# Retention and a snake feed-forward on one core: idle matmuls thinned among the first tiles, two clearings and a table in other gaps, the third sequence's q loads and turn moved

## The chip, the cores and the metric

The kernel runs on one core of a Trainium2 chip. The time is that of one execution on the device in microseconds, the median of several runs. The profile is taken in a separate execution, whose own time stands beside its span.

## The reference

Retention over B = 4 sequences of S = 768 tokens with H = 8 heads of D = 64, then a feed-forward over all 3072 tokens. Inputs and outputs are float32.

```python
gamma = 1.0 - 2.0 ** (-5.0 - np.arange(H))
for t in range(S):
    state = gamma[None, :, None, None] * state + np.einsum('bhd,bhe->bhde', k[:, :, t], v[:, :, t])
    y[:, :, t] = 1/np.sqrt(D) * np.einsum('bhd,bhde->bhe', q[:, :, t], state)
x = y.transpose(0, 2, 1, 3).reshape(B * S, H * D)      # 3072 x 512
h = x @ w_in                                           # 512 -> 2048
s = np.sin(alpha * h)
out = (h + s * s / (alpha + 1e-09)) @ w_out            # 2048 -> 512
```

## The kernel before

**Tiles.** The recurrence is cut into 24 chunks of 128 tokens, six for each sequence, held in bf16. `order` (`P`) begins with the first chunk of each of the four sequences, called `e0` to `e3`, which need no earlier state; then come chunks 1 to 5 of the first sequence, of the second, the third (P[14] to P[18]) and the fourth. The feed-forward takes the chunks in groups: the first four as group 0, then ten groups of two.

**One chunk.** q and k are turned (on PE for the first chunks by `half_T` and `stage_T`, with a copy out of PSUM by ACT or DVE; later by a transposing DMA on SP's queue, `turn`). `stage_A` makes the scores of q and k on PE, and DVE multiplies them with a mask or the table `dec`. `stage_M` multiplies them with v and adds what the state gives; the result goes to `xT`. `scale_v` multiplies the chunk's v in place by a decay, on POOL, after the products that need it unscaled; `stage_S` and `state` sum the state from it. From the second sequence's second remaining chunk on, "wide" chunks do the same in `burst`, on quarters of PE's array.

**Feed-forward.** A `Slot` multiplies `w_in` with `xT` into `ph` (L567), ACT takes the sine (L570) and its square (L575) or DVE the square, and DVE forms `gT` (L582). `ff_out` multiplies `gT` with `w_out` into `po` (L592); `take` copies it out and stores it from SP (L607).

**Order.** The order of the work on every engine is the order of the program's statements; `tc.manual_schedule()` keeps it. Each engine takes its instructions one after the other, and so does each queue: a load issued by POOL stands behind POOL's tables and scalings, a turn on SP behind the stores. Loads from POOL convert float32 to bf16 on the way; there are eight semaphores for them, so that a load waits for the eighth before it.

**The head.** The code from line 645 to 687 brings e0, e1 and e2 through `half_T`, `stage_A` and `stage_M`, with `idle_work` between the steps: matmuls of a cleared float32 tile `warm` into a PSUM tile `spare` that nobody reads, in units of 128 columns, at most four units in one matmul (the trace shows each of them as a pair). `grow(p)` makes the quarter p of `qg[:, 0]`, a table of decays, on ACT; `decay_table(c)` multiplies the whole of `qg[:, 0]` with `step` (1 on DVE, 2 and 3 on POOL, L223). `s_bd` are two tiles for the state that are cleared on DVE (L648). The last lines of the head are POOL's:

```python
    scale_v(e0, nc.gpsimd)
    decay_table(2, nc.gpsimd)
    decay_table(3, nc.gpsimd)
    load_chunk(e3)
    load_w_out(0)
    load_w_in(2)
```

Group 0's feed-forward follows in an order written out by hand (L754 to L897), which begins with `w_in`'s first two quarters and comes to `w_out`'s first at `F(1, 0, 2)`.

**The groups after.** `phase(g, ...)` runs group g in eight slots of two feature tiles; between them stand the output products of group g - 1 and what `atts[g]` has for the slot: (g, n) is slot n of group g. `score[n]` is the place where the scores of chunk P[n] are made: (3, 1) for P[11], (3, 5) for P[12], (4, 1) for P[13], (4, 5) for P[14]. `turns[n]` is the place of its transposing DMA; P[14]'s stands at `score[13]`. `load_seq(2, ...)` loads the third sequence's chunks 1 to 5 with one DMA for each head and tensor; in POOL's order (L784 to L809) its q loads come after the scalings of e2, P[10] and P[11].

Of the kernel before, what the change touches and what calls it, by code (L numbers as in the profile page):

```python
# [9 lines left out]
BF16 = mybir.dt.bfloat16  # L10
# [5 lines left out]
def kernel(  # L16
# [15 lines left out]
    nc = tc.nc  # L32
    B, H, S, D = q.shape
# [69 lines left out]
    def wide(j):  # L103
        return j >= NCH + 2 and j % NCH > 0

    def load_seq(bt, names="qkv", hs=range(H)):

        cs = [c for c in range(NCH) if wide(bt * NCH + c)]
        nh = 2 * len(cs)
        if "q" in names and hs[0] == 0:  # L110
            raw["seq", bt] = (big.tile([128, nh, 2, NP, D], BF16, name=f"qk_seq{bt}"),
                              big.tile([128, nh, NP, D], BF16, name=f"v_seq{bt}"))
        tqk, tv = raw["seq", bt]
        for name, src in (("q", q), ("k", k), ("v", v)):
            if name not in names:
                continue
            for h in hs:
                r = slice(64 * (h // NP), 64 * (h // NP) + 64)
                x = h % NP ^ h // NP
                o = tv[r, :, h % NP, :] if name == "v" else tqk[r, :, "qk".index(name), x, :]  # L120
                nc.gpsimd.dma_start(out=o, in_=src[bt, h, cs[0] * C:, :].rearrange("(f i) d -> i f d", i=64))  # L121
        for i, c in enumerate(cs):
            j, f = bt * NCH + c, slice(2 * i, 2 * i + 2)
            raw["qk", j], raw["k", j], raw["v", j] = tqk[:, f], tqk[:, f, 1], tv[:, f]
# [26 lines left out]
    def scale_v(j, eng):  # L151
        t, by = raw["v", j], kg
        if wide(j):
            t, by = t.rearrange("i f p d -> i (f p) d"), kgq
        eng.tensor_mul(t, t, by[:, j % NCH, :, None].to_broadcast([128, H, D]))  # L155
# [7 lines left out]

    warm = consts.tile([128, 512], F32, name="warm")
    nc.vector.memset(warm, 0.0)  # L165
    tiny = consts.tile([128, 1], F32, name="tiny")
    nc.scalar.activation(out=tiny, in_=warm[:, 0:1], func=ACTF.Exp)
    lg = consts.tile([128, H], F32, name="lg")
# [60 lines left out]
    s_bd = [big.tile([128, NP, 128], BF16, name=f"s_bd{i}") for i in range(2)]  # L229
# [9 lines left out]
    def turn_half(j, i, pt):  # L239

        t = raw["qk"[i], j]
        for p in range(NP):
            if i == 0 and paired(j):
                for f in range(2):
                    for e in range(2):
                        r = slice(64 * e, 64 * e + 64)
                        nc.tensor.transpose(pt[r, p, 64 * f:64 * f + 64], t[:, 2 * p + e, f, :], ident[:64, :64])
            else:
                nc.tensor.transpose(pt[:, p, :], t[:, 2 * p:2 * p + 2, :].rearrange("p h d -> p (h d)"), ident)  # L249

    def half_T(j, i, eng):

        if i == 0:
            st["qkT", j] = work.tile([128, 2 * NP, 128], BF16, name="qkT", tag="qkT", bufs=6)
        pt = psum.tile([128, NP, 128], BF16, name="pt", tag="mm", bufs=4)
        turn_half(j, i, pt)
        leave_T(j, i, pt, nc.scalar.copy if eng is nc.scalar else nc.vector.tensor_copy)

    def leave_T(j, i, pt, copy):

        o = st["qkT", j][:, i * NP:(i + 1) * NP, :]
        if i == 0 and paired(j):
            o = o.rearrange("d p (i f) -> d p f i", f=2)
            pt = pt.rearrange("d p (f i) -> d p f i", f=2)
        copy(o, pt)
# [39 lines left out]
    def stage_S(j):  # L305
        c = j % NCH
        if c == 0:
            st["ps"] = psum.tile([128, NP, D], F32, name="ps", tag="ps")
        ps = st["ps"]
        for p in range(NP):  # L310
            for e in range(2):
                nc.tensor.matmul(ps[64 * e:64 * e + 64, p, :], raw["k", j][:, 2 * p + e, :], raw["v", j][:, 2 * p + e, :],  # L312
                                 start=(c == 0 and p == 0), stop=True, skip_group_check=True)
        return ps
# [6 lines left out]
    def stage_M(j, tag="ty"):  # L321
        c = j % NCH
        g, i = place[j]
        if g not in xT:
            xT[g] = work.tile([128, KS, sizes[g] * C], BF16, name="xT", tag="xT", bufs=3)
        qkT, aT, vs = st["qkT", j], st["aT", j], raw["v", j]
        py = psum.tile([128, NP, 128], F32, name="py", tag=tag)
        if c > 0:
            for p in range(NP):
                for e in range(2):  # L330
                    r = slice(64 * e, 64 * e + 64)
                    nc.tensor.matmul(py[r, p, :], s_bd[c % 2][:, p, r], qkT[:, p, :],  # L332
                                     start=(p == 0), stop=True, skip_group_check=True)
        for p in range(NP):
            for e in range(2):
                nc.tensor.matmul(py[64 * e:64 * e + 64, p, :], vs[:, 2 * p + e, :], aT[:, e, p, :],  # L336
                                 start=(c == 0 and p == 0), stop=True, skip_group_check=True)
        x = xT[g][:, :, i * C:(i + 1) * C]
        if c == 0:
            nc.scalar.copy(x, py)  # L340
            return
        ps = stage_S(j) if c < NCH - 1 else None
        nc.vector.tensor_mul(x, py, qg[:, c])
        if ps is not None:
            if wide(j + 1):
                swapped(s_b[(c + 1) % 2][0], ps, nc.scalar.copy)
                swapped(s_f[0], ps, nc.vector.tensor_copy)
            else:
                keep_S(j, ps)
# [3 lines left out]
    def halves_M(j):  # L353

        g, i = place[j]
        aT, vs = st["aT", j], raw["v", j]
        for h, (tag, copy) in enumerate((("ps", nc.scalar.copy), ("ty", nc.vector.tensor_copy))):
            idle_work(2 * h)
            py = psum.tile([128, 2, 128], F32, name="py", tag=tag)
            for n in range(2):  # L360
                for e in range(2):
                    p = 2 * h + n
                    nc.tensor.matmul(py[64 * e:64 * e + 64, n, :], vs[:, 2 * p + e, :], aT[:, e, p, :],
                                     start=(n == 0), stop=True, skip_group_check=True)
            copy(xT[g][:, 2 * h:2 * h + 2, i * C:(i + 1) * C], py)
# [4 lines left out]
    def swapped(o, ps, copy):  # L370

        m = NP // 2
        copy(o[:, :m], ps[:, :m])
        for e in range(2):
            copy(o[half(1 - e), m:], ps[half(e), m:])
# [256 lines left out]
    spare = {"ps": psum.tile([128, 512], F32, name="spare", tag="mm", bufs=4)}  # L632

    def idle_work(n):
        while n > 0:
            m = min(n, 4) * 128
            nc.tensor.matmul(spare["ps"][:, :m], warm[:, :128], warm[:, :m], start=True, stop=True)  # L637
            n -= 4

    def grow(p):  # L640
        nc.scalar.activation(out=qg[:, 0, p, :], in_=tio, func=ACTF.Exp, scale=lgp[:, p:p + 1], bias=cscale)


    P = order
    e0, e1, e2, e3 = P[:B]
    idle_work(8)
    for t in s_bd:
        nc.vector.memset(t, 0.0)  # L648
    nc.vector.tensor_copy(raw["q", 0], near["q"])
    half_T(e0, 0, nc.scalar)  # L650
    half_table(0)
    nc.vector.tensor_copy(raw["k", 0], near["k"])
    half_table(1)
    idle_work(3)
    half_T(e0, 1, nc.vector)
    nc.scalar.activation(out=kg, in_=expo, func=ACTF.Exp, scale=-1.0)
    later_tables()
# [5 lines left out]
    grow(1)  # L663
    half_T(e1, 0, nc.scalar)
    nc.scalar.activation(out=kgq, in_=expoq, func=ACTF.Exp, scale=-1.0)
    grow(2)
    idle_work(2)
    half_T(e1, 1, nc.vector)
    nc.tensor.transpose(pal, alpha_row, ident_f)
    nc.scalar.copy(alpha_sb, pal)  # L670
    stage_M(e0)
    stage_A(e1)
    idle_work(2)
    grow(3)
    half_T(e2, 0, nc.scalar)
    idle_work(2)
    half_T(e2, 1, nc.vector)
    nc.scalar.activation(out=tiny, in_=warm[:, 0:1], func=ACTF.Sin)
    stage_M(e1)
    idle_work(1)  # L680
    stage_A(e2, 2)
    idle_work(3)
    halves_M(e2)
    idle_work(3)
    nc.vector.tensor_scalar_add(rec_alpha, alpha_sb, 1e-9)
    nc.vector.reciprocal(rec_alpha, rec_alpha)
    decay_table(1, nc.vector)
# [104 lines left out]
    scale_v(P[9], nc.gpsimd)  # L792
    load_seq(1, "v", range(4, H))
    scale_v(e2, nc.gpsimd)
    for j in P[10:12]:
        scale_v(j, nc.gpsimd)
    load_seq(2, "q")
    scale_v(P[12], nc.gpsimd)
    load_seq(2, "k")
    scale_v(P[13], nc.gpsimd)  # L800
# [97 lines left out]
    score = {6: (1, 1), 7: (1, 3), 8: (2, 0), 9: (2, 2), 10: (2, 5)}  # L898
# [5 lines left out]
    turns = {8: (1, 0), 9: (1, 2), 10: (1, 7), **{n + 2: score[n] for n in range(9, NJ - 2)}}  # L904
# [8 lines left out]
    for n in range(6, NJ + 1):  # L913
# [9 lines left out]
                at(score[n], SK(first))  # L923
        if n >= 18 and n + 1 < NJ:
            at(score[n], lambda j=P[n + 1]: scale_v(j, nc.gpsimd))
    turns[14] = score[13]
    for n, spot in sorted(turns.items()):
        at(spot, X(P[n]))
    phase(1, out_pieces(0, (3,)), atts[1], 2, (0, 6))
# [33 lines left out]
```

## Time and profile before

| | |
|---|---|
| median of 3 runs | 210.32 us (210.24 to 211.41) |
| profiled execution, own time | 211.66 us |
| its span | 209.9 us |
| PE, DVE, ACT, POOL busy | 97%, 76%, 76%, 52% of the span |
| chain that ended last | PE 88%, DMA 6%, POOL 3%, DVE 1% |
| first product with `w_out` on PE | 24.27 us after the span's start |
| idle matmuls (L637) | 22 records, 10.3 us |
| granted clock | 1.00 |

PE's busy time counts from a matmul's start to its modelled end, so a high share alone does not say that PE is at its best; but it says where PE waited. Times in the text count from the span's start. L and a number name a line of the kernel before.

### The profile page before, as it was taken

The numbers are of one execution on the slowest core, as the hardware profiler recorded it, in microseconds if no ns is written. First come the engines' busy times: TensorE is split into PE (matmuls) and PEld (weight loads), VectorE is DVE, ScalarE is ACT, GpSimd is POOL, SyncE is SP. The second block draws the span as 40 slices with busy tenths as digits, with TensorE's granted clock in tenths as the row PEclk, the third lists the DMA queues.
The fourth block names the chain that finished last, engine by engine and source line by source line (L and its number), as shares of the span: only waits on it lengthen the run. The fifth ranks groups of instructions, "written<-read, shape, count | busy, mean of one in ns | idle before, by whom it ended". The sixth has DMA issues, their size and how long they took to land.

```text
span 209.9 us, 5990 instructions
## 1 busy us (share of the span) xinstructions
PE 203.1 (97%) x2427; PEld 132.4 (63%) x2427; DVE 159.5 (76%) x363; ACT 159.6 (76%) x344; POOL 109.6 (52%) x148
## 2 busy tenths in 40 slices
PE   7899799999999999999999999999999999999994
PEld 2555554457766766766666667667666666666653
DVE  7868879876988788788798787788888778686540
ACT  7667698538999778888878888886877787888821
POOL 8799333899979739999679963000423101000000
PEclk9999999999999999999999999999999999999999
DMA  8999999999999999999999994403315110110112
GB/s 126 156 200 130 184 207 193 155 194 189 144 138 100 165 140 140 174 110 157 116 162 195 165 151 105 100 17 86 87 46 77 53 49 4 50 53 0 50 53 100
DMA packets 98747, 24.78 MB, mean 118 GB/s; under 512 B 91280, under 2 KB 95776, under 8 KB 98720
## 3 DMA queue, kind: packets, MB, share of 16 engines
q0 software_dynamic: 75968, 13.38, 84.9%
q1 hardware_dynamic: 22608, 10.96, 26.4%
q8 instruction: 19, 0.31, 0.6%
q10 hardware_dynamic: 144, 0.07, 0.1%
q14 instruction: 8, 0.07, 0.1%
HBM read 27.27 MB, written 6.29 MB: 160 GB/s over the span
## 4 chain that ended last, share of the span: by engine, by line
PE 88%; DMA 6%; POOL 3%; DVE 1%; issue 0%; SPq 0%; POOLq 0%
PE po L592 39%; PE ph L567 37%; DMA w_out<-in_moe_w_out_dram 4%; DMA o_sb<-in_k_dram 2%; PE poh L617 2%; PE py L397 2%; PE pa L293 1%; PE py L510 1%; PE py L332 1%; PE pt L249 1%; POOL qg L223 1%; PE pa L413 1%; PE py L336 1%; PE pa L433 1%; PE ps L312 1%; POOL vr L155 0%
## 5 line engine op out<-in xcount | busy, mean ns | idle before, releaser
L582 DVE SCALAR_TENSOR_TENSOR gT<-s,rec_alpha,ph 128x256 bf16<-128x256 f32 (+3 forms) x184 | 82.0, 488 | 26.5 <-ACT s L575 25.5
L570 ACT ACTIVATE s<-ph,alpha_sb 128x256 f32<-128x256 f32 (+3 forms) x184 | 79.1, 481 | 30.1 <-PE ph L567 29.1
L567 PE MATMUL ph<-xT,w_in 128*128 128x256 bf16 (+3 forms) x736 | 98.5, 277 | 0.0
L592 PE MATMUL po<-w_out,gT 128*128 128x512 bf16 x368 | 95.2, 380 | 0.7 <-DMA w_out<-in_moe_w_out_dram 0.7
L567 PEld LDWEIGHTS <-w_in 128*128 128x128 bf16 x736 | 70.6, 98 | 30.2 <-issue 0.4
L575 ACT ACTIVATE s<-s 128x512 f32<-128x512 f32 (+1 forms) x91 | 56.4, 623 | 2.6
L592 PEld LDWEIGHTS <-gT 128*128 128x128 bf16 x368 | 34.0, 98 | 26.5 <-issue 0.7
L438 POOL CAST s_b<-s_f 128x256 bf16<-128x256 f32 x10 | 4.0, 399 | 38.8 <-DVE s_f L462 21.0
L155 POOL TENSOR_TENSOR v_seq<-v_seq,kgq 128x512 bf16<-128x512 bf16 x14 | 14.7, 1070 | 8.6 <-issue 4.7
L121 POOL DMA_DIRECT2D qk_seq<-in_q_dram x24 | 17.1, 743 | 3.5 <-DMA v_seq<-in_v_dram 2.8
L121 POOL DMA_DIRECT2D qk_seq<-in_k_dram x24 | 17.1, 749 | 1.3 <-DMA qk_seq<-in_q_dram 1.3
L604 DVE COPY o_sb<-po 128x512 f32<-128x512 f32 x19 | 13.1, 690 | 5.4 <-PE po L592 5.3
L121 POOL DMA_DIRECT2D v_seq<-in_v_dram x24 | 17.1, 772 | 0.0
L637 PE MATMUL spare<-warm 128*128 128x256 f32 (+3 forms) x22 | 10.3, 563 | 1.5 <-DVE warm L165 1.5
L98 POOL DMA_DIRECT2D vr<-in_v_dram x10 | 9.1, 913 | 4.9 <-DMA w_out<-in_moe_w_out_dram 2.6
L421 DVE TENSOR_TENSOR aTw<-pa,maskq 128x512 bf16<-128x512 f32 (+1 forms) x14 | 10.1, 722 | 0.2
L98 POOL DMA_DIRECT2D qkr<-in_k_dram x9 | 8.1, 899 | 3.1 <-DMA w_out<-in_moe_w_out_dram 2.9
L528 DVE TENSOR_TENSOR xT<-py,qg 128x256 bf16<-128x256 f32 x26 | 9.7, 413 | 0.0
L155 POOL TENSOR_TENSOR vr<-vr,kg 128x512 bf16<-128x512 bf16 x8 | 8.7, 1088 | 1.4 <-PE py L336 1.4
L577 DVE TENSOR_TENSOR s<-s 128x512 f32<-128x512 f32 (+1 forms) x7 | 4.4, 633 | 4.5 <-ACT s L570 4.5
L98 POOL DMA_DIRECT2D qkr<-in_q_dram x6 | 5.3, 891 | 3.9 <-DMA w_in<-in_moe_w_in_dram 2.1
L302 DVE TENSOR_TENSOR aT<-pa,mask 128x1024 bf16<-128x1024 f32 x6 | 7.3, 1216 | 0.0
(110 smaller groups left out, 153.4 us busy)
## 6 DMA issues: line engine op xcount, KB each, us to landing
out_dram<-o_sb SPq DMA_DIRECT2D x23, 256.0 KB, 3.0
w_in<-in_moe_w_in_dram POOLq DMA_DIRECT2D x4, 512.0 KB, 10.0
w_out<-in_moe_w_out_dram POOLq DMA_DIRECT2D x4, 512.0 KB, 14.0
vr<-in_v_dram POOLq DMA_DIRECT2D x10, 128.0 KB, 6.6
qk_seq<-in_q_dram POOLq DMA_DIRECT2D x16, 80.0 KB, 6.0
qk_seq<-in_k_dram POOLq DMA_DIRECT2D x16, 80.0 KB, 5.0
v_seq<-in_v_dram POOLq DMA_DIRECT2D x16, 80.0 KB, 5.4
qkr<-in_k_dram POOLq DMA_DIRECT2D x9, 128.0 KB, 7.1
```

Source lines behind the costliest of these rows:

```text
L98: nc.gpsimd.dma_start(out=t, in_=chunk_of(src, j))
L121: nc.gpsimd.dma_start(out=o, in_=src[bt, h, cs[0] * C:, :].rearrange("(f i) d -> i f d", i=64))
L155: eng.tensor_mul(t, t, by[:, j % NCH, :, None].to_broadcast([128, H, D]))
L421: nc.vector.tensor_mul(aT.rearrange("p e m t -> p e (m t)").rearrange("p e (n t) -> p e n t", t=t), pa[:, :, 0:2 * n].rearrange("p e (n t) ...
L528: nc.vector.tensor_mul(x[:, 2 * b:2 * b + 2, :], y.rearrange("p (m t) -> p m t", m=2), qg[:, c, 2 * b:2 * b + 2])
L567: nc.tensor.matmul(self.ph[:, m, :], w_in[:, i, f * 128:(f + 1) * 128], xT[g][:, i, self.lo:self.hi], start=(m == 0 and i == 0), stop=(i = ...
L570: nc.scalar.activation(out=self.s[:, m, :], in_=self.ph[:, m, :], func=ACTF.Sin, scale=alpha_sb[:, f:f + 1])
L575: nc.scalar.activation(out=self.s, in_=self.s, func=ACTF.Square)
L582: nc.vector.scalar_tensor_tensor(gT[self.g][:, f, self.lo:self.hi], self.s[:, m, :], rec_alpha[:, f:f + 1], self.ph[:, m, :], op0=ALU.mult ...
L592: nc.tensor.matmul(po[g, ts], gT[g][:, f, ts * C:(ts + 1) * C], w_out[:, f, :], start=(f == 0), stop=(f == FF - 1))
L604: nc.vector.tensor_copy(o_sb, po[g, ts])
L637: nc.tensor.matmul(spare["ps"][:, :m], warm[:, :128], warm[:, :m], start=True, stop=True)
```

## The change

- `idle_work(n)` now uses one float32 matmul for 3 or 4 units, and a bf16 matmul of 512 columns for each single unit of what is left, on the same cleared memory (`warm16`). The numbers of units change: 8, 3, 2, 2, 2, 2, 1, 3, 2 (inside `halves_M`), 3 become 6, 4, 2, none, 1, 1, 1, 3, 1 (inside), 2, some of them at other places.
- The two clearings of `s_bd` leave the start and follow e1's and e2's turned k on DVE.
- `half_T(e1, 1)` comes before `grow(2)`; both of e2's turns come before `grow(3)`, which ran ahead of them.
- Six of the third sequence's eight q loads are issued before the scalings of P[10] and P[11] instead of after them.
- P[14]'s turn moves from (4, 1) to (3, 7).

```diff
+    warm16 = warm.bitcast(BF16)
...
-            idle_work(2 * h)
+            idle_work(h)
...
-            m = min(n, 4) * 128
-            nc.tensor.matmul(spare["ps"][:, :m], warm[:, :128], warm[:, :m], start=True, stop=True)
-            n -= 4
+            x, m = (warm, min(n, 4)) if n > 2 else (warm16, 4)
+            nc.tensor.matmul(spare["ps"][:, :m * 128], x[:, :128], x[:, :m * 128], start=True, stop=True)
+            n -= 4 if n > 2 else 1
...
-    idle_work(8)
-    for t in s_bd:
-        nc.vector.memset(t, 0.0)
+    idle_work(6)
...
-    idle_work(3)
+    idle_work(4)
     half_T(e0, 1, nc.vector)
...
     half_T(e1, 0, nc.scalar)
     nc.scalar.activation(out=kgq, in_=expoq, func=ACTF.Exp, scale=-1.0)
+    half_T(e1, 1, nc.vector)
+    nc.vector.memset(s_bd[0], 0.0)
     grow(2)
-    idle_work(2)
-    half_T(e1, 1, nc.vector)
     nc.tensor.transpose(pal, alpha_row, ident_f)
     nc.scalar.copy(alpha_sb, pal)
+    idle_work(1)
     stage_M(e0)
     stage_A(e1)
-    idle_work(2)
+    idle_work(1)
+    half_T(e2, 0, nc.scalar)
+    half_T(e2, 1, nc.vector)
+    nc.vector.memset(s_bd[1], 0.0)
     grow(3)
-    half_T(e2, 0, nc.scalar)
-    idle_work(2)
-    half_T(e2, 1, nc.vector)
     nc.scalar.activation(out=tiny, in_=warm[:, 0:1], func=ACTF.Sin)
+    idle_work(1)
     stage_M(e1)
-    idle_work(1)
     stage_A(e2, 2)
     idle_work(3)
     halves_M(e2)
-    idle_work(3)
+    idle_work(2)
...
     scale_v(e2, nc.gpsimd)
+    load_seq(2, "q", range(6))
     for j in P[10:12]:
         scale_v(j, nc.gpsimd)
-    load_seq(2, "q")
+    load_seq(2, "q", range(6, H))
...
-    turns[14] = score[13]
+    turns[14] = (3, 7)
```

## The prediction

> **What bounds the kernel now.** I began with the page's first part, then cut the execution into stretches by windows.
>
> ```profile
> span 209.9 us, 5990 instructions
> PE 203.1 (97%) x2427; PEld 132.4 (63%) x2427; DVE 159.5 (76%) x363; ACT 159.6 (76%) x344; POOL 109.6 (52%) x148
> ```
>
> ```profile
> 25.00:47.00 22.00, 21.86 (x196) 11.49 (x195) 18.07 (x34) 14.41 (x30) 12.95 (x16) 1.00 1.80 188
> 47.00:120.00 73.00, 73.00 (x994) 50.51 (x989) 58.33 (x125) 61.23 (x134) 63.50 (x84) 1.00 1.80 151
> 120.00:199.00 79.00, 79.00 (x993) 53.51 (x994) 60.66 (x141) 63.30 (x132) 12.91 (x21) 1.00 0.35 62
> ```
>
> The first pair of numbers is the length of the stretch and PE's busy time. From 47 us on PE is busy for all of it, before that for all but 0.14 us back to 25 us. So whatever begins PE's dense part early or late moves the end one for one, and nothing later can be won where no wait stands. What begins it is in PE's waits and in the chain of waits, read up to 24 us:
>
> ```profile
> PE po L592 <- DMA w_out<-in_moe_w_out_dram: 0.7, 1, 0.7
> ```
>
> ```profile
> 1.26 4.50 DMA o_sb<-in_k_dram
> 5.78 0.95 DVE kb L652
> ...
> 9.66 0.43 PE py L336 x8
> ...
> 10.24 1.04 POOL vr L155
> 11.28 1.99 POOL qg L223 x2
> 13.27 0.70 POOL qp L91
> 13.97 0.89 POOL qkr L98
> 14.86 0.85 POOL vr L98
> 15.71 8.52 DMA w_out<-in_moe_w_out_dram
> ```
>
> The first product with `w_out` starts at 24.27, when its first quarter lands (15.71 + 8.52 = 24.23). PE had waited 0.7 us for it. That load is issued by POOL behind a queue: the scaling of e0's v (waits for e0's `stage_M` on PE), two decay tables, three loads of e3's chunk. Before them POOL idled 1.39 us. So the start of the dense part is set by e0's chain and by POOL, not by how quickly PE gets through e1 and e2.
>
> **The change, part by part.** *e0's chain does not move.* `kb` starts when k has landed, 1.26 + 4.50 = 5.76; the clearings that leave DVE (0.55 us at 4.21) stood before that. `qb` can start at 4.21, since q landed 3.2 us after its issue at 0.74, so e0's q is turned at about 4.75 instead of 5.22, but its partner, k's turn, still comes at 6.79. The opening block of idle matmuls is now one 512-column fp32 and two bf16 instead of two fp32: less PE work before 4.75, on nobody's path. The four units between q's and k's turn lie before `kb`'s end at 6.73. The two after k's turn (0.65 us now, 2 x 0.22 as bf16 by the dense rows of L592, 0.86 us for 4) lie before DVE's copy of the turned k, which ends at 7.82. `stage_A(e0)`, its mask on DVE (8.39 to 9.62) and `stage_M(e0)` at 9.66 follow as before: the mask's end plus the 0.05 us that DVE's other hand-overs to PE take is 9.66, so taking idle work away in front of it on PE gains nothing. e1's k turn comes half a microsecond earlier, but its copy waits on DVE for that mask.
>
> *The clearings.* The first (half of 0.55 = 0.27 us) falls into DVE's 0.50 us of idle ahead of e1's mask at 10.45; the second comes after e2's k copy, before e2's mask has its scores. Cost nothing; without those gaps 0.27 us each on a path that ends in a wait anyway.
>
> *The table `grow(3)`.* This is the part I hold to decide. ACT and POOL now:
>
> ```profile
> 10.12 0.58 ACT L340 CAST xT<-py 128x512 bf16<-128x512 f32 x1 [0.16 <-PE py L336]
> 10.60 0.49 ACT L641 ACTIVATE qg<-tio,cscale,lgp 128x128 f32<-128x128 f32 x1
> 11.45 0.73 ACT L265 COPY qkT<-pt 128x512 bf16<-128x512 bf16 x1 [0.36 <-PE pt L247]
> 12.20 1.28 ACT L678 ACT_TABLE_LOAD   x1
> ```
>
> ```profile
> 10.24 1.04 POOL L155 TENSOR_TENSOR vr<-vr,kg 128x512 bf16<-128x512 bf16 x1 [1.39 <-PE py L336]
> 11.24 2.03 POOL L223 TENSOR_TENSOR qg<-qg,step 128x512 f32<-128x512 f32 x2
> ```
>
> `grow(3)` fills ACT's gap from 10.60 to 11.09, just before POOL's decay tables, which read all four quarters of `qg[:, 0]`. Moved behind `half_T(e2, 0)`, it stands behind ACT's copy of e2's turned q. That turn starts at 10.97 now, after two fp32 units of idle work (from 10.34, 0.63 us); with one bf16 matmul (0.22) and the change-over (about 0.1) at 10.66. The copy shifts with it from 11.45 to 11.14 and takes 0.73; successive ACT rows overlap by 0.1, so `grow(3)` runs from about 11.77 to 12.26. With the 0.15 us that POOL took to follow PE (10.24 against 10.09) the tables start at 12.4 instead of 11.24: **1.15 us later**. Queued behind them on POOL: e3's three loads, `w_out` 0, and all later loads. ACT itself loses 0.05 us (its table load starts at 12.25 for 12.20).
>
> *What PE gains.* `stage_M(e1)` is freed of idle work and starts at the end of e1's mask, 11.7 for 12.19; e2's second half then waits for ACT's copy of e1's output, which starts at 13.66 behind the table load, and the first `ph` product starts about 0.7 us earlier, at 15.3 for 15.99. All of this ends in waits: the second quarter of `w_in` (first used at 17.78 now), e3's q (5.3 us from issue to landing, so 13.22 + 1.15 + 5.3 = 19.7, for a turn at 19.33 now), and then `w_out`. e3's `stage_M` comes at 23.2 to 23.5, still ahead of `w_out`.
>
> *What the late issue costs.* Lower bound 0: if the rings were full, a later issue would land at the same time. That does occur: the four `w_out` loads, issued 0.7 to 1.5 us apart, take 8.5 to 17.6 us to land, so the later ones queue. Upper bound 1.15: landing follows issue. I take 1.0, near the upper end, because e3's q, right ahead of `w_out` in the queue, landed 5.3 us after its issue, and the median of all three such loads is that same 5.3: no backlog ahead of `w_out` 0. Everything behind it on the rings shifts alike, and PE with it.
>
> *Third sequence.* POOL idles 4.72 us ahead of its scaling at 76.79, waiting for v to land. Six q loads (0.72 us each, 5.76 for 8) fit in there, 72.1 to 76.4; the scaling still starts at 76.8 and all of the third sequence's loads end 4.3 us earlier. The turn of P[14] went out on SP at 94.86 behind the output store; PE reads its result at 103.83. Moved to (3, 7) it stands ahead of that store on SP and waits there for k, whose last issue moves from 90.4 to 86.2, so it goes out at about 90, before the store at 94. PE has no wait here to lose: 0. If k came after 94.2, the store would be late, and through `o_sb`'s three buffers DVE and PE.
>
> **Sum.** 0 (e0's chain) + 1.0 (POOL late) + 0 (PE's gain, spent in the wait for `w_out`) + 0 (third sequence) = +1.0 us on a span of 209.9. That execution took 211.66 in all, 1.34 above the median of the runs shown, 210.32; I carry the difference to the median: **211.3 us**.
>
> **Rivals.** *1. Not slower: the rings' rate, not the issue, sets the landing of `w_out` 0.* The four weight loads that queue speak for it; the constant 5.3 us speaks against. It decides if the rings are still busy with `w_in` and e3 when the delayed descriptors come, some 1.5 us after the issue ends at 17.6: `w_out` lands at 24.2, PE's gain is lost in its wait of then 0.7 to 1 us, and the time is 210.3. If in an undisturbed run `w_out` landed before PE came (23.4), PE's 0.7 us could show: 209.6.
>
> *2. Slower still: PE's slow start lasts longer.* The first idle matmuls ran at a lower pace:
>
> ```profile
> 1.46 3.67 PE L637 MATMUL spare<-warm 128*128 128x512 f32 x4 [1.46 <-DVE warm L165]
> 5.46 0.86 PE L637 MATMUL spare<-warm 128*128 128x384 f32 x2
> 7.02 0.65 PE L637 MATMUL spare<-warm 128*128 128x256 f32 x2
> ```
>
> A pair costs 0.21 us more per 128 columns, so 512 would cost 1.07; the first two pairs took 1.84 each. In the new order PE works from 1.46 to about 4.3 and then idles till 4.75. If the quick pace came only after another stretch of work, at about 8.3, the four units would last 1.84 instead of 1.07 and push k's turn to 7.2, the two bf16 units 0.86 instead of 0.43, and `stage_A(e0)` to 8.5 for 7.88: e0's chain, POOL and `w_out` 0.65 us later on top of my 1.0, 212.0. Against it: 2.8 of the first 3.3 us stay busy. The Trainium skill (TensorE: Matmul & The Clock Gate, "What's actually happening") says that PE runs at half its clock until one window of about 3.4 us has been busy, and that the window runs free of the kernel's start; 1.46 + 3.4 = 4.9 agrees with the trace's change between 4.2 and 5.2. By that rule a window with a hole in it may not count, and the time would be the 212.0 of this rival; the trace of before has no such hole and can't tell.
>
> *3. The turn or the scaled v of the second sequence comes late.* POOL's 4.72 us of idle speaks against; if the six loads overran by 2 us, the scaling for PE's burst at 80.43 would miss it, and each microsecond more is one on the end: about 213.
>
> **How the numbers follow.** Forecast 0.55, rival 1 0.24 (of it 0.05 for 209.6), rival 2 0.14, rival 3 0.04, others 0.03. A change under 1% (2.1 us) can't be told well from none in this kernel's measurement. The forecast is inside it, and so is nearly all of the rest: faster 0.03, since only the 0.7 us of PE's early gain are to be had; slower by over 1% (above 212.4) 0.10, from rival 3 and the upper part of rival 2. The range, 209.6 to 212.6, reaches from PE's whole gain to rival 2 with the full 1.15; the likeliest case's own is 210.8 to 211.6.
>
> **What would show it.** Right: POOL's decay tables at 12.4, `w_out` 0 issued at 16.9 and landing near 25.3, PE's wait before its first `po` grown from 0.7 to 1.5 us or more, `stage_M(e0)` still at 9.66. Wrong: tables before 11.5, or `w_out` landing by 24.3 in spite of its late issue (rival 1); k's turn after 7.0 (rival 2); a PE wait between 76 and 110 (rival 3); PE busy throughout from 47 is the sign for the third sequence's zero.

## The result and the profile after

The changed kernel is slower: 212.66 us median of 7 runs (212.04 to 214.2) against 211.08 us of 7 runs of the kernel before (210.24 to 211.41), a ratio of 1.0081, 95% interval 1.0051 to 1.011, that is 1.7 us (1.1 to 2.3). The forecast was slower by 1.0 us, 211.3, with a range to 212.6: the direction held, the size did not, and the time lies just above the range. The two profiled executions differ by only 0.9 us in span, since that of before took 0.6 us more than its kernel's median. Of the runs further down one execution of `e4`, 214.10 us at a granted clock of 0.984, is in the slow state and left out of its ratio.

The page's first part and the three stretches, read as before (length, then PE's busy time):

```profile
span 210.8 us, 5975 instructions
PE 202.7 (96%) x2421; PEld 130.8 (62%) x2421; DVE 159.1 (75%) x363; ACT 159.6 (76%) x344; POOL 109.7 (52%) x148
```

```profile
25.00:47.00 22.00, 21.20 (x171) 10.63 (x169) 17.33 (x33) 14.56 (x30) 11.33 (x13) 1.00 1.76 189
47.00:120.00 73.00, 72.93 (x942) 50.45 (x941) 57.79 (x124) 60.61 (x133) 68.59 (x91) 1.00 1.90 154
120.00:199.00 79.00, 79.00 (x1052) 53.44 (x1051) 61.44 (x141) 63.24 (x132) 9.04 (x15) 1.00 0.28 59
```

PE's idle time between 25 and 47 us grew from 0.14 to 0.80 us; behind 47 it is still next to nothing (0.07 us). PE's waits over the whole execution (us in all, times, the longest):

```profile
PE ph L568 <- DMA w_in<-in_moe_w_in_dram: 1.5, 3, 0.6
PE po L593 <- DMA w_out<-in_moe_w_out_dram: 0.8, 2, 0.7
```

Both name weight loads; before there was one such wait, of 0.7 us. Not all of that is the table's cost: two of the three waits for `w_in` (0.56 us ahead of 15.52, 0.41 ahead of 18.06) are for its first two quarters, which POOL issues ahead of the tables, and PE comes earlier to the first. ACT and POOL in the head of the changed kernel:

```profile
9.97 0.58 ACT L341 CAST xT<-py 128x512 bf16<-128x512 f32 x1 [0.16 <-PE py L337]
11.00 0.73 ACT L266 COPY qkT<-pt 128x512 bf16<-128x512 bf16 x1 [0.44 <-PE pt L248]
11.59 0.49 ACT L642 ACTIVATE qg<-tio,cscale,lgp 128x128 f32<-128x128 f32 x1
12.10 1.28 ACT L678 ACT_TABLE_LOAD   x1
```

```profile
10.10 1.04 POOL L155 TENSOR_TENSOR vr<-vr,kg 128x512 bf16<-128x512 bf16 x1 [1.14 <-PE py L337]
12.16 2.04 POOL L224 TENSOR_TENSOR qg<-qg,step 128x512 f32<-128x512 f32 x2 [1.02 <-ACT qg L642]
14.13 0.75 POOL L91 DMA_DIRECT2D qp<-in_q_dram  x1
16.62 0.78 POOL L134 DMA_DIRECT2D w_out<-in_moe_w_out_dram  x1
```

`grow(3)` (L642) stands behind ACT's copy of e2's turned q, and POOL idles 1.02 us for it between the scaling of e0's v and the decay tables, where before the tables followed without a gap. The loads behind them go out later: the first quarter of `w_out` at 16.62, where the profile of before has 15.71. In this execution that quarter landed after 7.2 us, so that `po` began at 23.85, 0.42 earlier than in the profile of before; the loss showed at `w_in`'s fourth quarter instead (issued at 18.83, landing 14.2 us later, at 33.0, where before it was 17.92 and 14.0, at 31.9):

```profile
33.09 1.90 PE L568 MATMUL ph<-xT,w_in 128*128 128x512 bf16 x8 [0.50 <-DMA w_in<-in_moe_w_in_dram]
```

PE turns P[4] at 40.15 instead of 39.47. Between 24 and 40 us it thus went from 0.42 us ahead to 0.68 behind; 0.66 us of these 1.1 are named as waits for weight loads.

### The profile page after: what moved, and what is told of

Same layout as the page of the kernel before. It is cut to its first block, busy times and chain, and to the rows that moved or that the text cites. A ratio compares the mean times of both kernels' runs of the same rounds, so it can differ in the third digit from the quotient of the medians.

```text
span 210.8 us, 5975 instructions
## 1 busy us (share of the span) xinstructions
PE 202.7 (96%) x2421; PEld 130.8 (62%) x2421; DVE 159.1 (75%) x363; ACT 159.6 (76%) x344; POOL 109.7 (52%) x148
## 4 chain that ended last, share of the span: by engine, by line
PE 82%; DMA 7%; DVE 4%; POOL 3%; ACT 2%; issue 1%; DVEq 0%
PE po L593 36%; PE ph L568 33%; DMA w_in<-in_moe_w_in_dram 7%; PE poh L618 2%; PE py L398 2%; PE pt L250 1%; ACT s L571 1%; PE pa L294 1%; PE spare L638 1%; PE py L511 1%; POOL qg L224 1%; PE pa L414 1%; PE py L333 1%; PE pa L434 1%; PE py L337 1%
## 5 line engine op out<-in xcount | busy, mean ns | idle before, releaser
L638 PE MATMUL spare<-warm 128*128 128x512 bf16 (+2 forms) x16 | 8.6, 620 | 1.5 <-DVE warm L165 1.5
```

The lines of the kernel that those rows point to most:

```text
L638: nc.tensor.matmul(spare["ps"][:, :m * 128], x[:, :128], x[:, :m * 128], start=True, stop=True)
```

## The experiments

The theory: the whole change in time is `grow(3)`'s late place, which holds POOL's decay tables and with them every load queued behind. The rivals: the thinner idle work, which prolongs PE's slow start (the prediction's rival 2), and the third sequence's loads and turn (rival 3). All kernels were timed beside runs of the kernel before, whose medians were 211.07 to 211.15 us.

| run | median us | ratio to before, 95% |
|---|---|---|
| the change | 212.66 | 1.0081 (1.0051 to 1.0110) |
| `e1` change, table put back | 211.12 | 1.0001 (0.9977 to 1.0025) |
| `e2` before, table moved alone | 213.02 | 1.0104 (1.0066 to 1.0143) |
| `e3` before, third sequence alone | 210.91 | 0.9997 (0.9974 to 1.0019) |
| `e4` idle work and clearings alone | 211.18 | 1.0002 (0.9976 to 1.0027) |
| `e5` before, POOL 1 us late | 212.23 | 1.0052 (1.0029 to 1.0076) |
| `e6` before, POOL 2 us late | 214.36 | 1.0136 (1.0108 to 1.0163) |
| `e7` before, loads first | 210.97 | 0.9985 (0.9969 to 1.0001) |
| `e8` change, loads first | 210.74 | 0.9986 (0.9972 to 1.0001) |
| `e9` `e6` with PE kept busy | 213.08 | 1.0103 (1.0073 to 1.0133) |
| `e10` change, table back, loads first | 210.45 | 0.9962 (0.9946 to 0.9979) |
| `e11` `e10`, tiles 3 and 4 exchanged | 210.32 | 0.9968 (0.9943 to 0.9992) |
| `e12` `e7`, tiles 3 and 4 exchanged | 210.88 | 0.9982 (0.9961 to 1.0002) |

**The parts.** `e1` undoes one line's place in the changed kernel:

```diff
     idle_work(1)
+    grow(3)
     half_T(e2, 0, nc.scalar)
     half_T(e2, 1, nc.vector)
     nc.vector.memset(s_bd[1], 0.0)
-    grow(3)
```

> The changed kernel with grow(3) put back ahead of half_T(e2, 0); all else as changed. Table theory (POOL's decay tables wait for grow(3), so that e3's and all weight loads are issued some 0.9 us later, and PE then waits for them): the tables start at 11.2 to 11.3 again, the second half of w_in and of w_out lands about 0.9 us earlier than in the changed kernel, and the time falls by 1 to 1.6 us, to that of before or up to 0.5 us below. Start-up theory (the thinner idle work lengthens PE's slow pace): 0 to 0.3 us of the 1.6 come back. Third-sequence theory: 0 to 0.3 us come back.

The loss is gone, within 0.5 us either way. In its profile the tables follow the scaling without a gap again:

```profile
9.53 1.04 POOL L155 TENSOR_TENSOR vr<-vr,kg 128x512 bf16<-128x512 bf16 x1 [0.46 <-PE py L337]
10.54 2.03 POOL L224 TENSOR_TENSOR qg<-qg,step 128x512 f32<-128x512 f32 x2
```

`e2` moves the same line in the kernel before, and nothing else:

```diff
-    grow(3)
     half_T(e2, 0, nc.scalar)
     idle_work(2)
     half_T(e2, 1, nc.vector)
+    grow(3)
```

> The kernel before with grow(3) moved behind half_T(e2, 1) and nothing else. Table theory: e2's turned q is still copied at 11.45 there, so the tables start at about 12.7 for 11.24, 1.45 us later, and the time rises by 1.4 to 2.2 us. Start-up and third-sequence theories: within 0.4 us of before.

Measured: 2.2 us slower (1.4 to 3.0), with POOL's gap in the profile:

```profile
11.80 2.04 POOL L223 TENSOR_TENSOR qg<-qg,step 128x512 f32<-128x512 f32 x2 [1.33 <-ACT qg L641]
```

`e3` has the hunks on `load_seq(2, ...)` and `turns[14]` of the change alone, `e4` the rest of the change without them and with `grow(3)` in its old place:

> The kernel before with the third sequence's q loads and P[14]'s turn moved as in the change and nothing else. Third-sequence theory: 0.6 to 1.6 us slower, with PE waits between 76 and 145 us. Table and start-up theories: within 0.3 us of before, PE busy throughout from 47 us.

> The changed kernel with grow(3) put back and the third sequence as before, so that idle matmuls, clearings and e1's and e2's k turn remain of the change. Start-up theory: 0.6 to 1.6 us slower than before, with e0's k turned after 6.8. Table and third-sequence theories: the time of before or up to 0.5 us less, since PE reaches its waits earlier without ending them earlier.

Neither differs from before; both intervals hold 1 and end within 0.3%. So of the parts the table alone has a cost that these runs can tell, in either kernel; the other parts neither win nor lose more than 0.6 us.

**Is it the lateness of POOL's loads?** In `e5` and `e6` the order on PE, ACT and DVE is that of before, and only POOL has more to do. The added line stands once in `e5` and twice in `e6`:

```diff
     decay_table(2, nc.gpsimd)
+    decay_table(2, nc.gpsimd)
     decay_table(3, nc.gpsimd)
```

> The kernel before with decay_table(2) written once more on POOL (the same values again), so that only POOL's loads come later, by one such row, 1.0 us; PE, ACT and DVE keep their order. Table theory with a landing that follows the issue: 0.7 to 1.1 us slower. Ring theory (the rings are busy and the landing stays): within 0.3 us of before. If the changed kernel's 1.6 us had another source than the late issue, this run would also stay near before.

> The same with two more writes of decay_table(2): POOL's loads 2.0 us later. Table theory: 1.6 to 2.2 us slower, twice the run with one. Ring theory: within 0.5 us of before. A slope above 1 (2.5 us or more) would say that a late issue costs more than its lateness.

The tables' rows in `e5` and in `e6`, where the kernel before has two in 2.03 us:

```profile
10.43 3.15 POOL L223 TENSOR_TENSOR qg<-qg,step 128x512 f32<-128x512 f32 x3
```

```profile
11.47 4.27 POOL L223 TENSOR_TENSOR qg<-qg,step 128x512 f32<-128x512 f32 x4
```

So the loads are held 1.1 and 2.2 us longer. That costs 1.1 us (0.6 to 1.6) in `e5` and 2.9 (2.3 to 3.4) in `e6`. In both the first quarter of `w_out` landed 8.5 us after its issue, as in the profile of before: it follows the issue. `e6` costs more than twice `e5` by its middle value, though the intervals also allow twice; a reason stands in the profile of `e6`. PE's work around the wait, and stretches of it (the last three numbers of each are granted clock, DMA share and GB/s):

```profile
26.71 1.24 PE L592 MATMUL po<-w_out,gT 128*128 128x512 bf16 x5 [2.85 <-DMA w_out<-in_moe_w_out_dram]
27.79 3.53 PE L567 MATMUL ph<-xT,w_in 128*128 128x128 bf16 x32
```

```profile
27.00:28.00 1.00, 1.00 (x8) 0.53 (x7) 0.00 (x0) 0.00 (x0) 0.83 (x1) 0.94 1.23 205
28.00:29.00 1.00, 1.00 (x13) 1.00 (x11) 0.00 (x0) 0.00 (x0) 0.00 (x0) 0.50 1.24 207
29.00:30.00 1.00, 1.00 (x12) 1.00 (x11) 0.00 (x0) 0.36 (x2) 0.11 (x1) 0.50 1.26 208
30.00:31.00 1.00, 1.00 (x12) 1.00 (x10) 0.18 (x1) 0.78 (x4) 0.78 (x1) 0.50 1.21 203
31.00:32.00 1.00, 1.00 (x7) 0.55 (x6) 0.96 (x3) 0.65 (x3) 0.00 (x0) 0.86 1.30 221
```

After 2.85 us without work the granted clock falls to 0.50 for 3.4 us ((0.06 + 3 x 0.5 + 0.14) / 0.5), and the 32 products at L567 take 3.53 us where they took 1.95 in the changed kernel. `e9` is `e6` with work in that wait:

```diff
     po[0, 1] = psum.tile([128, d_model], F32, name="po", tag="ty")
+    spare2 = psum.tile([128, 512], F32, name="spare2", tag="ps")
+    for _ in range(8):
+        nc.tensor.matmul(spare2, warm.bitcast(BF16)[:, :128], warm.bitcast(BF16)[:, :512], start=True, stop=True)
     F(1, 0, 2)
```

> POOL's loads 2.0 us late as in the run with two more table writes, and eight bf16 idle matmuls of 512 columns (8 x 0.22 = 1.7 us) on PE right before the first product with w_out, so that PE's wait there is cut from 2.85 us to about 1.1. Clock theory (the loss of 2.9 us for 2.0 us of lateness is 2.0 us of late landing and the rest a granted clock of 0.50 for 3.4 us after the long wait): granted clock 1.00 throughout and 1.5 to 2.3 us slower than before. If the clock has no part in the median, the loss stays at 2.5 to 3.2 us.

```profile
25.41 1.24 PE L592 MATMUL po<-w_out,gT 128*128 128x512 bf16 x5 [0.65 <-DMA w_out<-in_moe_w_out_dram]
```

```profile
24.00:27.00 3.00, 2.35 (x19) 1.24 (x18) 1.39 (x3) 0.00 (x0) 0.88 (x1) 1.00 1.23 201
```

The granted clock is 1.00, PE's wait 0.65 us, and the loss 2.2 us (1.5 to 2.8) instead of 2.9. (The load also landed 1.3 us earlier than in `e6`'s profile; with the 1.89 us of added work the wait would have been some 2.5 us, an estimate.) The clocks of the single executions say the same: three of `e6`'s six have a mean of 0.992 and took 214.57 to 215.72 us, the other three have 1.00 and took 212.73 to 214.15, and none of `e9`'s six is below 0.998. Still the two intervals overlap, so the clock's share of the median, some 0.7 us, is likely rather than settled; that it fell in `e6`'s profiled execution is shown. The Trainium skill (TensorE: Matmul & The Clock Gate, "What's actually happening") says that half rate returns after an idle window of about 3.4 us; here 2.85 us of idling were enough, and the measurement decides. In the changed kernel the longest such wait of the profile is 0.7 us and the clock stays at 1.00; of its seven executions one, of 214.2 us, shows 0.992. So do two of `e2`'s six (214.26 and 214.51); the median of its other four is 1.4 us above before, that of all six 1.9. Of the 82 executions of the kernel before that were timed beside the experiments none is below 0.998. The late table is not needed for such a fall, since two of `e4`'s twelve and one of `e11`'s show 0.984 to 0.991.

**Loads first.** If the late table costs through the queue behind it alone, it must be free once nothing waits behind it. `e7` (on the kernel before), `e8` (on the change) and `e10` (on `e1`) move three lines:

```diff
-    scale_v(e0, nc.gpsimd)
-    decay_table(2, nc.gpsimd)
-    decay_table(3, nc.gpsimd)
     load_chunk(e3)
...
     load_w_out(3)
+    scale_v(e0, nc.gpsimd)
+    decay_table(2, nc.gpsimd)
+    decay_table(3, nc.gpsimd)
```

> The kernel before with POOL's scaling of e0's v and its two decay tables moved behind load_w_out(3): e3's and the weights' loads wait for nothing of e0 any more and are issued from about 8.9 us on. Table theory: w_out's first quarter lands at 22 to 23.5 instead of 23 to 24.2, later weights 1 to 2 us earlier, PE's waits on w_in and w_out nearly vanish, 0.6 to 1.5 us faster. Ring theory: the rings are full until w_in's second quarter has landed at 17.7 anyway, gain at most 0.4 us.

> The changed kernel, its late grow(3) kept, with POOL's scaling of e0's v and the two decay tables moved behind load_w_out(3). If the late table costs through the loads queued behind it alone, all of the 1.6 us goes, and the time is that of the kernel before with the same move, within 0.5 us. If grow(3) behind e2's copy costs on ACT or PE too (its sine table load, e1's output), 0.5 us or more of the loss stays between the two.

> The changed kernel with grow(3) put back and POOL's scaling of e0's v and the two decay tables behind load_w_out(3). Table theory: with no load behind the tables, grow(3)'s place is free, so the time is that of the changed kernel with the loads first (0.3 us below before), within 0.3 us. If grow(3)'s late place still cost on ACT, 0.3 to 0.8 us faster than that.

`e8` is as fast as `e7`, 0.3 us below before, so nearly all of the 1.7 us is gone though the table is as late as in the change: its cost came through the queue behind it. Whether all of it is gone is not settled. `e10` and `e8` differ in the table's place alone, and `e10` is 0.3 us faster by the medians and 0.5 by the ratios, with intervals that just overlap; `e10`'s own expectation named 0.3 to 0.8 us as the sign of a cost on ACT. In the profiles of both PE waits for the first two quarters of `w_in` and reaches `po` at 22.74 and 22.77, so they show no such cost.

The gain over before is small, and for `e7` and `e8` not clear of none: the ring rival's at most 0.4 us held, the 0.6 to 1.5 of the table theory did not. `e8` issued the first `w_out` quarter here:

```profile
11.56 0.83 POOL L134 DMA_DIRECT2D w_out<-in_moe_w_out_dram  x1
```

That is 4.2 us earlier than the 15.71 of before, but the load took 11.1 us to land where it had taken 8.5, so it landed 1.6 us earlier. That the rings were still busy with `w_in` is the likely reason, not a shown one. `e10` is the only one of the three clear of before, 0.8 us below it (0.4 to 1.1).

**Another order behind the loads.** Of the remaining waits in `e8` one, of 0.40 us, is for `w_in`'s second quarter, so `e11` (on `e10`) and `e12` (on `e7`) put a tile of the first quarter ahead:

```diff
-    w[4] = early(4, "ps")
+    w[4] = early(3, "ps")
...
-    w[3] = early(3)
+    w[3] = early(4)
```

> The same, and group 0's feature tile 3, of w_in's first quarter, takes the early place of tile 4, of the second quarter, and tile 4 the later place of 3. PE's remaining wait, for w_in's second quarter (0.4 us of 1.0 at 17.7 in the changed kernel with the loads first), gets 4 x 0.16 = 0.65 us of other work ahead of it: 0.2 to 0.6 us faster than without, 0.5 to 1.0 us below before.

> The kernel before, its idle matmuls and clearings as they were, with the loads first and tiles 3 and 4 exchanged. If the thinner idle work is worth something once the loads wait for nothing, this is 0.2 to 0.6 us slower than the run with the changed head; if PE's early gain is again spent in a wait, the two agree within 0.2 us.

`e11` doesn't differ from `e10`, nor `e12` from `e7`: the exchange wins nothing that these runs can tell. `e10` is ahead of `e7` and `e11` of `e12` by 0.1 to 0.2%, with overlapping intervals, so whether the thinner idle work is worth something with the loads first stays open.

## Why the prediction was right or wrong

**Right: the mechanism and its place.** The table was named as the part that decides, through ACT's copy, POOL's tables and the loads behind them; `e1` and `e2` show the part, `e5`, `e6` and `e8` the way through the loads. ACT's rows come where they were put (`grow(3)` from 11.59 against 11.77, its sine table load at 12.10 against 12.25), the tables at 12.16 against 12.4. That they fit so well is partly luck: `stage_M(e0)` came at 9.53 for the 9.66 of the forecast, because k landed at 5.3 instead of 5.76 while PE's slow start lasted longer. In `e1`, with a quick start, the same step came at 8.96. The zeros of the clearings and of the third sequence hold (`e4`, `e3`): POOL's six q loads took 4.33 us of its idle time and the scaling started 0.75 us after them, when v had landed. P[14]'s turn went out at 93.28 rather than at about 90, still ahead of the store, at 94.98.

**Wrong: the time it was added to.** The prediction carried +1.0 us to the median of three runs, 210.32. Over 7 to 29 runs of the same kernel the median is 211.07 to 211.15. This alone is 0.8 us of the 1.4 us between 211.3 and 212.66. The profiled execution, 211.66, lay above all three runs, which was a sign that they ran low.

**Wrong: the size of the term "1.0 (POOL late)".** It measured 1.7 us (1.1 to 2.3) in the change, and 2.2 (1.4 to 3.0) with the table moved alone (`e2`). It was made of a lateness of 1.15 us and an effect a little below one for one. The effect is not shown to be below one: `e5` held the loads 1.1 us longer and cost 1.1 (0.6 to 1.6), `e6` 2.2 us longer and cost 2.9. The lateness was read off one profile, in which k landed at 5.76 and `kb` took 0.95 us, and it isn't fixed. In the twelve experiments k landed at 5.1 to 5.5. The tables of kernels with `grow(3)` in its place, which began at 11.24 in the profile of before, began at 10.43 to 10.60 in `e1`, `e3`, `e5` and `e9`, and at 11.32 and 11.47 in `e4` and `e6`, whose start was slow. `e1` and `e3` issued the first `w_out` quarter at 15.01 and 15.06, so the changed kernel's 16.62 is 0.9 us later than the profile of before, but 1.6 later than these, its own slow start included. A chain that starts earlier leaves POOL to wait longer for a table that hangs on e2's q: POOL's wait for `grow(3)` was 1.02 us in the changed kernel's profile and 1.33 in `e2`'s. One for one, such waits give 1.0 to 1.3 us, at the lower end of the measured interval. What is left up to its middle isn't settled.

**Wrong: where it would show.** `w_out` 0 was to land near 25.3 and PE's wait there to grow to 1.5 us; the wait was 0.67 us and the load landed at 23.8 in the profiled execution, although it was issued 0.9 us later than before; later weight loads were late instead. One profile of a kernel whose landings vary says little of which load will be the late one; the lateness of all of them is what counts.

**Rivals.** Rival 1 (the rings set the landing) is refuted for late loads by the times of `e5` and `e6`; early ones land later after their issue than it takes before (`e8`), as it said. Its 1.5 us from the end of an issue to the descriptors was too long: in the trace of before the first packets of POOL's first load come at 3.61, 1.15 us after its issue ends. Rival 2's slow start is real but belongs to both kernels: the two records of idle matmul ahead of k's turn took 1.17 and 1.04 us in the changed kernel's profile, 1.00 and 0.59 in `e1`'s, 0.54 and 0.49 before, but 0.96 and 0.85 in `e6`, which has the idle work of before. k's turn then comes at 6.8 to 7.0 instead of about 6.2. It is the clock: the trace's own clock record, before whose first entry the views count 1.00, has the full clock from 6.84 us on in the changed kernel's profile and from 4.89 in that of before. It begins at 6.61 to 7.39 in `e6`, `e11` and `e12`, and at 4.35 to 5.70 in `e1`, `e2`, `e3` and `e7` to `e10` (`e4` and `e5` have no record); of `e1`'s two records the slow one, 1.00 us, lies mostly ahead of its 5.70, the quick one, 0.59, behind it. The hole that the change leaves in PE's first work does not decide it: in `e1` PE idled 0.21 us ahead of q's turn at 4.60 and had the full clock at 5.70, while `e6` and `e12`, without that hole, had it at 7.39 and 6.61. `e4`'s median shows that the thinner work doesn't change the average. Rival 3 is refuted by `e3`.

## What to carry to other kernels

Follow a moved instruction to every engine that reads its result, not only along the engine whose gap it leaves or fills: here a 0.49 us table, moved to a quiet place on ACT, held a queue of loads on another engine, and the bill came 12 us and more later as a wait for weights. Loads that need nothing of the computation should not stand behind work that does: with the loads first the late table cost next to nothing, though the new order alone (`e7`) won nothing that its runs can tell. And take the base of a small difference from many runs, not from three and one profile.

## What was not expected

A wait of 2.85 us on PE was followed by 3.4 us at a granted clock of 0.50 (`e6`), so that a late load can cost more than its lateness. In that trace's clock record the full clock begins at 7.39 us, falls at 27.87 and is back at 31.28. The 20.48 us up to the fall are six times the 3.41 us that the fall lasted. This is one case; whether a fall comes only at such steps no run here shows.

The kernel's first 7 us differ from execution to execution: PE's quick pace began before or after the second block of idle work in either kernel, which moves e0's chain by up to 1 us (`stage_A(e0)` at 7.06 in `e5`, at 8.10 in `e6`, with the same order on PE).
